# A routed and a dense mixture of experts behind linear attention: order of weight requests, scatters and weight sums

## The chip, the cores and the metric

The kernel runs on one core of one Trainium2 chip. The metric is the device time of one execution in microseconds (us). All inputs and outputs are float32; where a product goes to TensorE, both factors are split into a high and a low part, and three matmuls (high x high, high x low, low x high) stand for one.

## The reference

Three layers follow one another; N = 2304 rows, D = 512 columns, E = 8 experts, F = 1024.

```python
x = attention(q, k, v, w_phi)            # linear attention, 2304 x 512
# moe: some rows are computed, each by one expert
do_compute = x @ w_skip > 0
e_idx = argmax(x[do_compute] @ w_gate, axis=1)
x[do_compute] += gate_w * (relu(x @ w1[e]) @ w2[e])     # e = e_idx of the row
# moe2: every row by every expert
P = exp(x @ w_gate - max); 8 times: normalise rows, then columns
for e in range(8):
    out += P[:, e:e + 1] * (relu(x @ w1[e]) @ w2[e])
```

## The kernel before, in words

**Attention** fills about the first 215 us and leaves x in a DRAM table `x2d`. A router (lines around 440 to 530) writes for every computed row its place in a list `idx` by nine scatters on POOL (`rt.scatter`, L456); the list is sorted by expert and cut into slots of 256 rows.

**moe1** (L561 to L777) works through the slots. In a slot `s` (`slot_body`, L650 on) POOL scatters the results of slot s-1 into `x2d`, in two halves of 128 rows (`put`, L715); SP reads the number of the next expert, the list of the next slot's rows (L586) and its w1 (L617); POOL gathers these rows (`fetch_x`, L597). TensorE makes the first product in eight pieces `ph` (L668), while ACT and DVE split w2 (L629, L630). Then `ahead` requests the next w2 and splits the next w1, `turned` transposes the next slot's rows on TensorE (L643) with copies on ACT (L645) and DVE (L646), and `product` makes the second product for half 0 and half 1 (L707), each ending in a DVE add into the gathered rows (L711). Slots 0 and 1 are always run. The slots from 2 on are nested conditions (`chain`, L730); in each, `ahead` and `turned` stand inside a condition on there being a next slot, and the second half of the product inside one on the slot being full (`tc.If(nfull > s - 2)`, L690). Slot 0 is put in order by a planner from the program order; slot 1 and all later ones run in the order in which they are written (`tc.manual_schedule`). In this data nine slots run; slots 7 and 8 are not full. After the last slot the Else branch of the chain scatters the last results, and 24 transposes on a constant (`warm`, L775) stand between it and moe2.

While moe1 runs, `ahead2()` takes single steps of moe2's beginning, in a fixed order: load w1 of the first quad (L818); make Strassen-like sums of it on POOL (`sums_w1`, three operations at L830 to L832); seven splits (`w1_high` on ACT, L842, `w1_low` on DVE, L848; the second split has one more POOL operation, L850); load w1 of the second quad. Before, the first step comes after `rt.scatter()`, the sums at the end of slot 0's `ahead`, four splits between slot 0's two products, three in slot 1, and the second load after slot 1.

**moe2** (L780 on) has three passes of 768 rows each over 16 quarters of experts; one pass and quarter is a `quad` (48 in all), and the passes run through the weights forth, back and forth, so a pass begins with the weights with which the last one ended. A quad has two groups (`group`, L1082). A group makes the hidden layer by seven products `pa`, `pb`, `pd` (L1031), with the additions on DVE (L1101, L1116) and copies on ACT (L1039, L1047), and the three `piece`s of the quad before (second product `py`, L1067, twelve matmuls for each piece and quarter-block) lie between them as fill. In group 0 ACT and DVE split this quad's w2 (`w2_high` L1017, `w2_low` L1022) in four blocks; in group 1 they split the next quad's w1. SP issues the loads: `load_w1` into one buffer, `load_w2` into two buffers `r2`, blocks 0 and 1 at the end of the quad before, blocks 2 and 3 as soon as blocks 0 and 1 are split. In the last pass's first quads SP also stores the finished rows (`out`, L1080); at the end of the second quad from a pass's end it loads the next pass's x. Quads 0 to 2 are ordered by the planner, all later ones run as written. The requests stand at the end of `quad`:

```python
                if g and more:
                    load_w1(wid[n + 1] + 1)
                    load_w2(wid[n + 1], 0)
                    load_w2(wid[n + 1], 1)
```

Before quad 0, moe2 loads six blocks of 128 rows (L886) and turns them (`x_block`): four transposes (L893) into one bank `pt` of two, from which ACT copies one half and DVE the other (L896, L897).

Of the kernel before, what the change touches and what calls it, by code (L numbers as in the profile page):

```python
# [11 lines left out]
U32 = mybir.dt.uint32  # L12
# [13 lines left out]
NTOK = B * S  # L26
# [534 lines left out]
def moe1(tc, nc, c, rt, w1, w2, idx, x2d, second, route, ahead2):  # L561

    with ExitStack() as ctx:
# [73 lines left out]
        def turned(s, ps0=None):  # L637
            xg, xT = xgs[s % 3], xTs[s % 2]
            for a in range(2):
                pt = (ps0.tile([P, NKB, P], F32, name="pt", tag="W", bufs=4) if ps0  # L640
                      else ps.tile([P, NKB, P], F32, name="pt", tag="T"))
                for kb in range(NKB):
                    nc.tensor.transpose(pt[:, kb], xg[:, a, kb * P : kb * P + P], c["ident"])  # L643
                oh, ol = [t[:, :, a * P : a * P + P] for t in xT]
                nc.scalar.activation(oh, pt, AF.Copy)  # L645
                nc.vector.tensor_tensor(ol, pt, f32(oh), ALU.subtract)  # L646
# [5 lines left out]
        def slot_body(s):  # L652
            xT = xTs[s % 2]
            last = s == NSLOT + 1
            if s:
                put(s - 1, (0, 1))
            if s == 0:
                e = e1
            elif not last:
                e = fetch(s + 1)  # L660
            hh = pool.tile([P, NFB, SLOT], F32R, name="hh", tag="hh", bufs=1)
            hl = pool.tile([P, NFB, SLOT], F32R, name="hl", tag="hl", bufs=1)
            for f in range(NFB):
                ph = ps.tile([P, SLOT], F32, name="ph", tag="H", bufs=3)
                n = 0
                for wt, xt in ((w1h, xT[0]), (w1h, xT[1]), (w1l, xT[0])):
                    for kb in range(NKB):
                        nc.tensor.matmul(  # L668
                            ph, wt[:, kb, f * P : f * P + P], xt[:, kb], start=(n == 0), stop=(n == 11)
                        )  # L670
                        n += 1
                nc.scalar.activation(hh[:, f], ph, AF.Relu)
                nc.vector.scalar_tensor_tensor(hl[:, f], ph, 0.0, f32(hh[:, f]), ALU.max, ALU.subtract)
                split_w(w2h[:, f], w2l[:, f], r2[:, f])
            if s < 2:
                ahead(s, e)
                if s == 0:
                    ahead2()
            elif not last:
                with tc.If(nslots > s - 1):  # L680
                    ahead(s, e)
                    turned(s + 1)
            product(s, 0, hh, hl)
            if s < 2:
                if s == 0:
                    turned(1)
                for _ in range(4 if s == 0 else 3):
                    ahead2()
                product(s, 1, hh, hl, (lambda: turned(2)) if s else None)
            else:  # L690
                with tc.If(nfull > s - 2):
                    product(s, 1, hh, hl)

        def ahead(s, e):
            fetch2(e)
# [3 lines left out]
        def product(s, a, hh, hl, between=None):  # L699
            xg = xgs[s % 3]  # L700
            py = ps.tile([P, D], F32, name="py", tag="Y")
            n = 0
            for f in range(NFB):
                if between and f == NFB // 2:
                    between()
                for ht, wt in ((hh, w2h), (hl, w2h), (hh, w2l)):
                    nc.tensor.matmul(  # L707
                        py, ht[:, f, a * P : a * P + P], wt[:, f], start=(n == 0), stop=(n == 23)
                    )
                    n += 1  # L710
            nc.vector.scalar_tensor_tensor(  # L711
                xg[:, a, 0:D], py, xg[:, a, D : D + 1], xg[:, a, 0:D], ALU.mult, ALU.add
            )

        def put(s, halves):  # L715
            ix, xg = ixs[s % 3], xgs[s % 3]
            for a in halves:
                ins = nc.gpsimd.indirect_dma_start(
                    out=x2d[:, :],
                    out_offset=bass.IndirectOffsetOnAxis(ap=ix[:, a].bitcast(U32), axis=0),  # L720
                    in_=xg[:, a],
                    in_offset=None,
                    bounds_check=NTOK - 1,
                    oob_is_err=False,
                )
                for o in rt.gathers + rt.written:
                    tc.declare_no_dep(ins.ins, o.ins, reason="distinct rows")
                rt.written.append(ins)

        def chain(s):  # L730
            if s <= NSLOT + 1:
                with tc.If(nslots > s - 2) as more:
                    slot(s)
                    chain(s + 1)
                with more.Else():
                    put(s - 1, (1, 0))
            else:
                put(s - 1, (1, 0))

        es = rt.early_slots()  # L740
        first = [next(es)]
# [20 lines left out]
        w2h, w2l = [pool.tile([P, NFB, D], F32R, name=nm, bufs=1) for nm in ("w2h", "w2l")]  # L762
        xTs.append([pool.tile([P, NKB, SLOT], F32R, name=nm, bufs=1) for nm in ("xTh1", "xTl1")])
        route(lambda: ps.tile([P, D], F32, name="pr", tag="Y"))
        rt.scatter()
        ahead2()
        tabs.extend(rt.slots())
        slot_body(0)
        slot(1)
# [2 lines left out]
        nfull = nc.values_load(tn[0:1, 0:1], min_val=0, max_val=NSLOT)  # L772
        nslots = nc.values_load(tn[0:1, 1:2], min_val=0, max_val=NSLOT)
        chain(2)
        for _ in range(24):  # L775
            nc.tensor.transpose(warm, c["ident"], c["ident"])  # L776
    yield  # L777

# [1 line left out]
def moe2(tc, nc, c, w_gate, w1, w2, x2d, xtd, out):  # L780
# [6 lines left out]
    with ExitStack() as ctx:  # L787
# [98 lines left out]
            nc.sync.dma_start(xr, row(t, 0))  # L886
            return xr

        def transposed(xr, dst):

            pt = ps.tile([P, NKB, P], F32, name="pt", tag="T", bufs=2)
            for kb in range(NKB):
                nc.tensor.transpose(pt[:, kb], xr[:, kb * P : kb * P + P], c["ident"])  # L893
            (d, s), *more = dst(pt)
            nc.scalar.activation(d, s, AF.Copy)
            for d, s in more:  # L896
                nc.vector.tensor_copy(d, s)  # L897

        def logits(ps_, h, src):

# [31 lines left out]

        def x_block(xr, h, i):
            sl = slice(i * P, i * P + P)
            transposed(xr, lambda pt: [(xq[h, kh][:, :, sl], pt[:, 2 * kh : 2 * kh + 2]) for kh in range(2)])

        def x_logits(h):
            logits(0, h, lambda kb: xq[h, kb // 2][:, kb % 2])
# [221 lines left out]
        def quad(n):  # L1160
            ps_, e, q = quads[n]
            nxt = n + 1 < NQD and quads[n + 1][0] != ps_
            near = n + 4 < NQD and quads[n + 4][0] != ps_ and quads[n + 3][0] == ps_
            fresh = n == 0 or wid[n] != wid[n - 1]
            more = n + 1 < NQD and wid[n + 1] != wid[n]
            for g in range(2):
                high, low = [none] * 7, [none] * 7
                if n == 0:
                    fill = [lambda i=i: other_logits(*others[2 * g + i]) if i < 2 else None for i in range(3)]
                else:  # L1170
                    fill = [lambda i=i: piece(n - 1, g, i) for i in range(TB)]
                if g == 0:
                    if more:
                        sums_w1(wid[n + 1])
                    if fresh:
                        for b, k in enumerate((0, 1, 4, 5)):
                            high[k] = lambda b=b: w2_high(wid[n], b)

                            def lo(b=b):
                                w2_low(wid[n], b)  # L1180
                                if b < 2:
                                    load_w2(wid[n], b + 2)

                            low[k] = lo
                    if nxt:
                        for i, k in enumerate((2, 3, 6)):
                            low[k] = lambda i=i: sum_x(i)
                elif more:
                    for k in range(7):
                        high[k] = lambda k=k: w1_high(wid[n + 1], k)  # L1190
                        low[k] = lambda k=k: w1_low(wid[n + 1], k)
                elif nxt:
                    for k in range(7):
                        high[k] = lambda k=k: x_high(k)
                        low[k] = lambda k=k: x_low(k)
                lead = [lambda: x_logits(0), lambda: x_logits(1)] if n == 0 and g == 0 else ()
                group(n, g, fill, high, low, lead)
                if g and more:
                    load_w1(wid[n + 1] + 1)
                    load_w2(wid[n + 1], 0)  # L1200
                    load_w2(wid[n + 1], 1)
                if near and g:
                    load_xt(ps_ + 1)
                if n == 0 and g:
                    sinkhorn_start()
                if 1 <= n <= 2:
                    sinkhorn_step()
                    sinkhorn_step()
# [115 lines left out]
```

## Time and profile before

| what | us |
|---|---|
| median of three runs | 1990.36 (1989.43 to 1997.06) |
| the profiled execution's own time | 1988.57 |
| its span | 1986.9 |
| around the span | 1.67 |
| TensorE busy in the span | 1945.5 (98%) |
| VectorE, ScalarE, GpSimd busy | 1263.2, 882.6, 354.1 |
| TensorE's share of the chain that ended last | 73% |
| mean granted TensorE clock | 0.992 of full speed |

PE is TensorE, DVE VectorE, ACT ScalarE, POOL GpSimd, SP SyncE, which issues most DMAs; SPq, PEq, POOLq are the engines' sequencers. A timeline row is: start in us from the span's start, duration of the run of equal instructions, engine, line, operation, tile written <- tiles read, shape, how many; in brackets the idle time of the engine just ahead and what ended it. In a window row the columns are: from : to, its length, busy time (and instructions) of PE, PEld, DVE, ACT, POOL, the granted clock (PEclk, share of full speed), the share in which the DMA engines were busy, and GB/s.

### The profile page before, as it was taken

The page shows a single profiled execution, that of the slowest core. Times are in us where ns is not written, and L with a number is a line of the kernel's source. Part 1 is how long each engine was busy: PE and PEld are TensorE (multiplying, and loading weights), DVE is VectorE, ACT ScalarE, POOL GpSimd, SP SyncE. Part 2 cuts the span into 40 slices and gives each one's busy share as a digit, 9 for nine tenths or more (in the row PEclk, how much of TensorE's full clock was granted, in tenths as well). Part 3 has the DMA queues.
Part 4 walks back from the last instruction along what each step waited for, and adds up shares of the span by engine and source line. Part 5 has one row for each costly group of instructions (what it writes and reads, how often), then busy time and mean ns, then how long its engine had stood idle before and what let it go on. Part 6 is the DMA issues. An engine that isn't in the chain of part 4 may idle for free.

```text
span 1986.9 us, 32388 instructions
## 1 busy us (share of the span) xinstructions
PE 1945.5 (98%) x12602; PEld 1738.5 (88%) x12602; DVE 1263.2 (64%) x2182; ACT 882.6 (44%) x1682; POOL 354.1 (18%) x293
## 2 busy tenths in 40 slices
PE   9989999989999999999999999999999999999999
PEld 8978889966889889898889889998888989899997
DVE  5767876764866666666555656666565666666663
ACT  5756555545444434343343434344334434434441
POOL 2020332221121221212021121212202121221210
PEclk9999999999999999999999999999999999999999
DMA  7324577645122221222112121222202121221211
GB/s 184 98 63 153 117 282 223 203 142 164 45 73 65 63 80 48 85 83 77 57 60 75 54 85 43 85 65 95 75 32 90 48 85 58 70 78 50 85 54 43
DMA packets 132711, 180.79 MB, mean 91 GB/s; under 512 B 22530, under 2 KB 86274, under 8 KB 132544
## 3 DMA queue, kind: packets, MB, share of 16 engines
q1 hardware_dynamic: 128768, 171.22, 27.4%
q0 software_dynamic: 3616, 7.30, 1.1%
q8 instruction: 102, 1.67, 0.4%
q14 instruction: 65, 0.53, 0.1%
q10 hardware_dynamic: 160, 0.07, 0.0%
HBM read 163.85 MB, written 17.69 MB: 91 GB/s over the span
## 4 chain that ended last, share of the span: by engine, by line
PE 73%; DMA 2%; DVE 2%; ACT 1%; SPq 0%; issue 0%; ACTq 0%
PE py L1067 37%; PE pb L1031 15%; PE pd L1031 10%; PE pa L1031 9%; DMA r<-in_moe_w_dram 2%; PE pg L903 1%; PE pt L893 0%; DVE wcl L848 0%; SPq L818 0%; ACT w2h L1017 0%; PE warm L776 0%; DVE w2l L1022 0%; DVE hl L1052 0%; DMA xr<-x2d 0%; DVE acc L1078 0%
## 5 line engine op out<-in xcount | busy, mean ns | idle before, releaser
L1067 PE MATMUL py<-w2l,hh 128*128 128x512 f32 x1152 | 452.1, 393 | 0.0
L1067 PE MATMUL py<-w2h,hh 128*128 128x512 f32 x1152 | 451.8, 392 | 0.0
L1067 PE MATMUL py<-w2h,hl 128*128 128x512 f32 x1152 | 451.2, 392 | 0.0
L1022 DVE TENSOR_TENSOR w2l<-r,w2h 128x512 fp32r<-128x512 f32 x184 | 176.2, 963 | 207.4 <-ACT w2h L1017 207.3
L1067 PEld LDWEIGHTS py<-w2l,hh 128*128 128x128 f32 x1152 | 216.6, 188 | 48.4
L1067 PEld LDWEIGHTS py<-w2h,hl 128*128 128x128 f32 x1152 | 216.7, 188 | 38.7 <-issue 1.3
L1067 PEld LDWEIGHTS py<-w2h,hh 128*128 128x128 f32 x1152 | 216.9, 188 | 36.2
L1078 DVE SCALAR_TENSOR_TENSOR acc<-py,lg,acc 128x512 f32<-128x512 f32 x264 | 197.1, 747 | 68.4 <-PE py L1067 67.6
L1047 ACT ACTIVATE hh<-c 128x384 fp32r<-128x384 f32 x192 | 100.9, 525 | 214.1 <-DVE c L1116 119.4
L1017 ACT ACTIVATE w2h<-r 128x512 fp32r<-128x512 f32 x184 | 114.3, 623 | 171.5 <-DMA r<-in_moe_w_dram 171.2
L850 POOL TENSOR_TENSOR r<-r,s 128x512 f32<-128x512 f32 x46 | 59.7, 1297 | 667.6 <-DVE wcl L848 667.6
L830 POOL TENSOR_TENSOR s<-r 128x512 f32<-128x512 f32 x46 | 59.2, 1287 | 569.8 <-DMA r<-in_moe_w_dram 568.7
L1031 PE MATMUL pb<-xch,wch 128*128 128x384 f32 x576 | 149.9, 341 | 7.9 <-ACT v L1039 6.5
L848 DVE TENSOR_TENSOR wcl<-r,wch 128x512 fp32r<-128x512 f32 x230 | 154.2, 686 | 2.3 <-ACT wch L842 1.8
L1031 PE MATMUL pb<-xch,wcl 128*128 128x384 f32 x576 | 148.0, 337 | 0.0
L1031 PE MATMUL pb<-xcl,wch 128*128 128x384 f32 x576 | 147.8, 337 | 0.0
L842 ACT ACTIVATE wch<-r 128x512 fp32r<-128x512 f32 x230 | 138.6, 622 | 7.3 <-PE pa L1031 2.9
L1101 DVE TENSOR_TENSOR pb<-pb,s 128x384 f32<-128x384 f32 x96 | 54.4, 566 | 121.9 <-PE pb L1031 65.3
L1031 PEld LDWEIGHTS pb<-xch,wch 128*128 128x128 f32 x576 | 105.4, 188 | 28.2 <-ACT v L1039 12.3
L1039 ACT ACTIVATE s<-pa 128x384 f32<-128x384 f32 x96 | 47.2, 491 | 175.8 <-PE pa L1031 175.8
L1052 DVE SCALAR_TENSOR_TENSOR hl<-c,hh 128x384 fp32r<-128x384 f32 x192 | 106.6, 555 | 6.1 <-ACT hh L1047 6.1
L848 DVE TENSOR_TENSOR wcl<-s,wch 128x512 fp32r<-128x512 f32 x92 | 64.8, 704 | 70.6 <-ACT wch L842 69.4
(237 smaller groups left out, 3573.2 us busy)
## 6 DMA issues: line engine op xcount, KB each, us to landing
r<-in_moe_w_dram SPq DMA_DIRECT2D x168, 512.0 KB, 3.6
r<-in_moe_w_dram SPq DMA_DIRECT2D x184, 256.0 KB, 4.1
qt<-in_q_dram SPq DMA_DIRECT2D x16, 288.0 KB, 5.1
x2d<-x SPq DMA_DIRECT2D x4, 1152.0 KB, 5.5
xr<-x2d SPq DMA_DIRECT2D x18, 256.0 KB, 3.7
out_dram<-acc SPq DMA_DIRECT2D x18, 256.0 KB, 2.1
kt<-in_k_dram SPq DMA_DIRECT2D x16, 256.0 KB, 4.5
vs<-in_v_dram SPq DMA_DIRECT2D x14, 256.0 KB, 3.9
```

The source lines that it names most:

```text
L830: g.tensor_tensor(s1, a21, a22, ALU.add)
L842: nc.scalar.activation(wc[m, i][0], wsrc[m][i], AF.Copy)
L848: nc.vector.tensor_tensor(l, src[i], f32(h), ALU.subtract)
L850: nc.gpsimd.tensor_tensor(src[3], src[2], src[6], ALU.subtract)
L1017: nc.scalar.activation(h, w2r[m, b], AF.Copy)
L1022: nc.vector.tensor_tensor(l, w2r.pop((m, b)), f32(h), ALU.subtract)
L1031: nc.tensor.matmul(dst, w[:, kb, sl], x[:, kb], start=(start and m == 0), stop=(stop and m == 5), skip_group_check=True,)
L1047: nc.scalar.activation(hh, src, AF.Relu)
L1052: nc.vector.scalar_tensor_tensor(hl, src, 0.0, f32(hh), ALU.max, ALU.subtract)
L1067: nc.tensor.matmul(py, ht[:, i * P : i * P + P], wt, start=(m == 0), stop=(m == 11))
L1078: nc.vector.scalar_tensor_tensor(accs[t], py, lg[:, t, e : e + 1], accs[t], ALU.mult, ALU.add)
L1101: v.tensor_tensor(b, b, s, ALU.add)
```

## The change

- In moe2, blocks 0 and 1 of the next quad's w2 are requested at the end of group 0 and not of group 1; `load_w1` stays at the end of group 1, and so now comes behind them.
- `put` scatters one half. The second half's scatter is issued right behind the second half's product, inside its condition (in slots 0 and 1 without one); the next slot, or the Else branch, scatters half 0 alone. In a slot that isn't full, half 1 is no longer scattered.
- The load and the sums of moe2's first w1 go ahead of the router's nine scatters. Slot 0 takes three splits (the second with its POOL operation), slot 1 four.
- In slot 2, `turned(3)` moves out of its condition and behind the first half's product.
- 16 warm transposes stand where 24 stood.
- In `x_block`, both copies of a block go to ACT or both to DVE, by turns.

```diff
@@ slot_body
             if s:
-                put(s - 1, (0, 1))
+                put(s - 1, 0)
...
             if s < 2:
                 ahead(s, e)
-                if s == 0:
-                    ahead2()
             elif not last:
                 with tc.If(nslots > s - 1):
                     ahead(s, e)
-                    turned(s + 1)
+                    if s > 2:
+                        turned(s + 1)
             product(s, 0, hh, hl)
             if s < 2:
                 if s == 0:
                     turned(1)
-                for _ in range(4 if s == 0 else 3):
+                for _ in range(3 if s == 0 else 4):
                     ahead2()
                 product(s, 1, hh, hl, (lambda: turned(2)) if s else None)
+                put(s, 1)
             else:
+                if s == 2:
+                    turned(3)
                 with tc.If(nfull > s - 2):
                     product(s, 1, hh, hl)
+                    put(s, 1)
@@ chain
                 with more.Else():
-                    put(s - 1, (1, 0))
+                    put(s - 1, 0)
             else:
-                put(s - 1, (1, 0))
+                put(s - 1, 0)
@@ moe1
+        ahead2()
+        ahead2()
         rt.scatter()
-        ahead2()
...
-        for _ in range(24):
+        for _ in range(16):
             nc.tensor.transpose(warm, c["ident"], c["ident"])
@@ x_block
+            if (h + i) % 2:
+                transposed(xr, to, nc.vector.tensor_copy)
+            else:
+                transposed(xr, to)
@@ quad
                 if g and more:
                     load_w1(wid[n + 1] + 1)
+                elif more:
                     load_w2(wid[n + 1], 0)
                     load_w2(wid[n + 1], 1)
```

## Rows read from the trace of the kernel before

**Rows 1.** The chain that ended last, in order of time: start, duration, engine.

```profile
571.61 2.76 PE py L1067 x12
587.21 2.76 PE py L1067 x12
...
996.83 2.29 PE pb L1031 x6
999.12 4.50 PE py L1067 x12
1003.62 1.06 PE pb L1031 x6
...
1943.46 2.76 PE py L1067 x12
```

**Rows 2.** Waits of PE after 500 us: total, count, longest.

```profile
PE pb L1031 <- ACT v L1039: 6.5, 5, 3.3
PE pd L1031 <- DVE c L1116: 2.0, 2, 1.0
```

**Rows 3.** Timeline of SP and ACT at quad 17, the second quad of the second pass.

```profile
978.76 9.00 SPq L1080 DMA_DIRECT2D out_dram<-acc  x3
...
988.92 10.24 SPq L1013 DMA_DIRECT2D r<-in_moe_w_dram  x4
...
995.76 0.63 ACT L1017 ACTIVATE w2h<-r 128x512 fp32r<-128x512 f32 x1 [7.52 <-DMA r<-in_moe_w_dram]
```

**Rows 4.** Timeline of a quad in mid-pass: w2 requests (SP), the last block's split (DVE).

```profile
1717.50 9.43 SPq L1013 DMA_DIRECT2D r<-in_moe_w_dram  x4
...
1731.94 0.68 DVE L1022 TENSOR_TENSOR w2l<-r,w2h 128x512 fp32r<-128x512 f32 x1
```

**Rows 5.** Timeline of slot 0: first and last list scatter, last weight sum, split; slot 1's first matmuls.

```profile
224.24 1.02 POOL L456 DMA_INDIRECT idx<-ids,di  x1 [46.15 <-DVE n L524]
...
235.31 1.42 POOL L456 DMA_INDIRECT idx<-ids,di  x1 [0.30 <-issue]
...
241.62 1.26 POOL L832 TENSOR_TENSOR r<-r 128x512 f32<-128x512 f32 x1
241.68 0.63 ACT L842 ACTIVATE wch<-s 128x512 fp32r<-128x512 f32 x1 [7.95 <-POOL s L831]
...
243.34 0.73 PE L668 MATMUL ph<-xTh,w1h 128*128 128x256 f32 x4 [2.11 <-ACT xTh L645]
```

**Rows 6.** Windows: the beginning of slot 1.

```profile
244.80:248.40 3.60, 3.60 (x21) 3.60 (x20) 3.60 (x5) 1.10 (x3) 1.56 (x1) 0.53 0.24 49
```

**Rows 7.** Timeline of slot 1: list of slot 2's rows (SP), slot 2's first matmuls (PE).

```profile
251.21 0.39 SPq L586 DMA_DIRECT2D ix<-idx  x1
...
268.63 0.72 PE L668 MATMUL ph<-xTh,w1h 128*128 128x256 f32 x4
```

**Rows 8.** Timeline: a gather and the transposes that use it, in slots 2 and 4.

```profile
274.63 1.10 POOL L597 DMA_INDIRECT xg<-x2d,ix  x1 [0.31 <-issue]
...
281.78 0.63 PE L643 MATMUL pt<-ident,xg 128*128 128x128 f32 x4 [0.50 <-DMA xg<-x2d,ix]
...
321.39 1.01 POOL L597 DMA_INDIRECT xg<-x2d,ix  x1 [0.31 <-issue]
...
328.05 1.04 PE L643 MATMUL pt<-ident,xg 128*128 128x128 f32 x8
```

**Rows 9.** Timeline of the end of moe1 and the beginning of moe2.

```profile
425.56 1.00 POOL L718 DMA_INDIRECT x2d<-xg,ix  x1 [0.31 <-POOLq L732]
427.55 5.17 PE L776 MATMUL warm<-ident 128*128 128x128 f32 x23 [4.51 <-PEq L732]
```

**Rows 10.** Windows: the warm transposes, and the transposes of x behind them.

```profile
427.50:432.70 5.20, 5.15 (x24) 5.16 (x25) 0.00 (x0) 0.00 (x0) 3.75 (x3) 0.50 0.60 176
432.70:436.00 3.30, 2.31 (x19) 1.82 (x18) 1.27 (x3) 1.88 (x4) 0.00 (x0) 0.99 1.05 380
```

**Rows 11.** Waits of PE from 400 to 445 us: total, count, longest.

```profile
PE pt L893 <- DVE xq L897: 1.2, 3, 0.5
```

More of the change, by code (lines that the diff above doesn't have):

```diff
@@ L713, in product, with put @@
             )
-        def put(s, halves):
+        def put(s, a):
             ix, xg = ixs[s % 3], xgs[s % 3]
[L717 to L728, printed above, removed]
+            ins = nc.gpsimd.indirect_dma_start(
+                out=x2d[:, :],
+                out_offset=bass.IndirectOffsetOnAxis(ap=ix[:, a].bitcast(U32), axis=0),
+                in_=xg[:, a],
+                in_offset=None,
+                bounds_check=NTOK - 1,
+                oob_is_err=False,
+            )
+            for o in rt.gathers + rt.written:
+                tc.declare_no_dep(ins.ins, o.ins, reason="distinct rows")
+            rt.written.append(ins)
         def chain(s):
@@ L887, in load_x, with transposed @@
             return xr
-        def transposed(xr, dst):
+        def transposed(xr, dst, copy=lambda d, s: nc.scalar.activation(d, s, AF.Copy)):
             pt = ps.tile([P, NKB, P], F32, name="pt", tag="T", bufs=2)
@@ L893, in transposed @@
                 nc.tensor.transpose(pt[:, kb], xr[:, kb * P : kb * P + P], c["ident"])
[L894 to L897, printed above, removed]
+            for d, s in dst(pt):
+                copy(d, s)
         def logits(ps_, h, src):
@@ L934, in x_block @@
             sl = slice(i * P, i * P + P)
-            transposed(xr, lambda pt: [(xq[h, kh][:, :, sl], pt[:, 2 * kh : 2 * kh + 2]) for kh in range(2)])
+            to = lambda pt: [(xq[h, kh][:, :, sl], pt[:, 2 * kh : 2 * kh + 2]) for kh in range(2)]
+            if (h + i) % 2:
+                transposed(xr, to, nc.vector.tensor_copy)
+            else:
+                transposed(xr, to)
         def x_logits(h):
```

## The prediction

> **What bounds the kernel now.** I read the page's busy times first: TensorE is busy for 98% of the span, so a change can only win in the stretches in which PE stands or runs at the lower clock, and three parts of this one touch such stretches. Next I read the chain that ended last [rows 1]. In moe2 its groups follow one another at 587.21 - 571.61 = 15.60 us. From the group at 571.61 to the last one, at 1943.46, there are 87 groups; 87 x 15.60 = 1357.2, and the trace takes 1371.85. So 14.65 us of moe2 are not the rhythm of PE, and the search is for where they lie. PE's waits after 500 us [rows 2] name two places: `pb` behind ACT's copy `v`, 6.5 us in five waits, and `pd` behind DVE's `c`, 2.0 us. The largest single wait, 3.3, is the one at quad 17. There the timeline of the queues [rows 3] gives the cause: SP first issues three stores of finished rows (from 978.76, over 9 us), and requests w2 at 988.92 only; ACT stands 7.52 us at the first w2 split, which runs at 995.76; the copy `v` is queued behind that split, and PE behind `v`. PE then pays twice. After the pause it runs at the lower clock: in [rows 1] twelve `py` take 4.50 at 999.12 against 2.76 elsewhere, and six `pb` 2.29 at 996.83 against 1.06 at 1003.62, together 3.0 us. A wait and its clock: 3.3 + 3.0 = 6.3 us at one place.
>
> **A: w2 requested in mid-quad.** It removes the late request. In a quiet quad [rows 4] the four w2 requests begin at 1717.50, at the start of the quad that needs them, and the last of the blocks is split at 1731.94 + 0.68 = 1732.6. There are two buffers, both free by then, so in the new order the next quad's first two requests can go out at about 1732.6, and the next quad begins 2 x 15.60 after 1717.50, at 1748.7: 16 us of lead instead of none. In quad 17 the request also goes ahead of the second three stores, and of `load_w1`, which is the only thing that is queued behind it. `load_w1` keeps its place and is first used by POOL's sums, later than w2 was. The same four blocks are moved, split by the same instructions; nothing is added on ACT or DVE. Gain: 6.3 at quad 17, 3.2 in the other four waits for `v`, 2.0 in those for `c` (DVE's w2 splits stand ahead of `c` and start late with ACT's), together 11.5; of the remaining 14.65 - 11.5 = 3.15, which no wait names, I take half, since the small losses can be ACT's late splits as well as anything else. **13.1 us**; bounds: 6.3 (only the pass boundary) and 14.65 (all).
>
> **B: weight sums ahead of the list.** Before, POOL issues nine scatters between 224.24 and 236.73, then the three sums up to 241.62 + 1.26 = 242.88, and ACT's first split of a sum waits 7.95 for them; the copy that slot 1's first matmul needs is queued behind it, and PE waits 2.11 at 243.34 [rows 5] and then works 3.6 us at a granted clock of 0.53 [rows 6], worth 3.6 x 0.47 = 1.7. The sums now come first (POOL stood idle for 46.15 before the first scatter, so there is room, if the weights have landed), and this pause of 2.11 + 1.7 = 3.8 goes; that is the upper bound. But slot 2 is tied to something else: its list is loaded at 251.21, when all scatters have landed, and its first matmul runs 17.42 later, at 268.63 [rows 7], with w1's load, its splits and the transposes in between. ACT has one split more in this stretch than before. If the list is complete when it was, most of the 3.8 is lost again in front of slot 2; if the sums push the scatters back by all their 242.88 - 236.73 = 6.15, the list is that much later, and with the 1.7 kept the part costs 4.4. I take **1.3**, a third of the upper bound, since the POOL had room; bounds -4.4 and 3.8.
>
> **C: turned(3) behind product 0.** Its transposes wait for the gathers: before the second four PE stands 0.50, and these four take 0.63 where eight take 1.04 in slot 4, which comes to 0.11 more [rows 8]. The same again for the first four gives 1.2; behind a product of 24 matmuls the rows have landed. **1.1**; bounds 0.5 and 1.2. What is next late there is nothing that the timeline shows.
>
> **Half scatters.** In a full slot the second half's scatter, which waits for DVE's last add, now goes ahead of the first half's, and the gathers come behind both. At worst they are 1.33 later (1.01 + 0.31, the pace of [rows 8]). A gather issued by 321.39 + 1.01 = 322.40 is used at 328.05, 5.65 later; 4.3 would be left. The longest landing that the rows allow is slot 2's, where the transposes did wait: 281.78 - (274.63 + 1.10) = 6.05. I cost the move at **nothing**, since the 4.3 is what is left behind the eight `ph` and w1's splits and no wait of PE shows in slot 4 now; but by the longest landing it would be 6.05 - 4.3 = 1.7 short in each of the five full slots, 8.7 us. The sequencer of POOL already followed that condition, so no branch is new to it.
>
> **D: the end of moe1.** The last slots aren't full, so one scatter less stands at the end: 1.31 on POOL (1.00 at 425.56 and 0.31 ahead of it), and the x loads, which wait for the last one, come that much earlier. PE's warm transposes take 5.17 / 23 = 0.22 each [rows 9]; eight fewer free 1.8, and the transposes of x move up by the smaller of the two with what slack the landing had: 1.5. In `x_block`, copies split by block and not by half let ACT and DVE work on different banks; PE waits 1.2 there [rows 11], of which I take 1.0. Against this stands the clock. While PE does nothing but these transposes, from 427.5 to 432.7, the granted clock is 0.50 (1.2 GHz), and in the next window, in which the x transposes go on, 0.99 (2.4 GHz) [rows 10]. If the warm ones are 1.5 us shorter and the rise stays where it is, that much of the x transposes runs at half speed, a loss of up to 0.75, of which 0.5 falls in PE's busy share (2.31 of 3.30). **2.0**; bounds 0.5 and 3.0 (1.8 + 1.2).
>
> The Trainium skill (TensorE: Matmul & The Clock Gate, Part 4: PE-mode transpose) says that transpose mode does not count as PE busy for the clock. By it the eight could be dropped without any price in clock, and part D would be 2.5 and not 2.0. The trace disagrees: its clock rose after 5.2 us in which PE did transposes alone.
>
> **Sum.** 13.1 + 1.3 + 1.1 + 0 + 2.0 = 17.5 us. The profiled execution took 1988.57; 1988.57 - 17.5 = 1971.1. The median of the runs is 1.79 above that execution, so on the median's basis **1972.9**. Attention, the normalisation of P and the tail are not touched.
>
> **The rivals**, on the same basis (1990.36):
> - *The list is late.* The sums, now first on POOL, push the nine scatters, and slot 2 starts some 4.4 us later than now instead of 1.3 earlier: 5.7 less gain, 1978.6. For it: three operations of 1.3 to 3.5 us stand in the same queue, and slot 2 follows its list at once. Against it: POOL had 46 us to spare. 0.14.
> - *Only the pass boundary was w2.* The small losses in the other quads come from something else: A gives 6.3, 1979.7. For it: four of five waits for `v` are 0.8 us on average; against it: ACT's w2 splits wait for the load in quad after quad. 0.08.
> - *Gathers uncovered.* Five full slots wait 1.7 each: 1981.4. Against it stands the 5.65 of [rows 8]. 0.04.
> - *The request is no earlier in fact*, because SP or a buffer holds it in mid-quad: A gives nothing, 1986.0. Against it is the free buffer at 1732.6. 0.04.
> - *Slower than before*: POOL stands at the first sum, waiting for moe2's first w1, whose load is in SP's queue behind moe1's, and nine scatters stand behind it. From the list load (251.21) slot 2 moves one for one. It decides from where B's loss eats the other 16.2 us, a list load after 267.4. With one 30 us late the time is 1990.36 + 30 - 16.2 = 2004.2. For it: one engine and one queue, and no way past a waiting operation; against it: the load is requested before the scatters too, and a w2 block lands in some 7 us even when late (988.92 to 995.76). 0.02.
>
> **How the numbers follow.** Forecast 0.68, rivals 0.14, 0.08, 0.04, 0.04, 0.02. All upper bounds together (14.65 + 3.8 + 1.1 + 3.0) give 1967.8, all lower ones (6.3 - 4.4 + 0.5 + 0.5) 1987.5. The low end is 1967.0, that and the 0.9 by which the fastest run lies under the median; the high end is 1982.0, which takes in the first three rivals and leaves out the last two and part of the mixtures. A measurement of this kernel can tell 0.5%, some 10 us, from no change: faster means under 1980.4. The forecast, the first rival and most of the second lie there, 0.84; a fifth of the first two, the uncovered gathers and the void request are within, 0.14; the last rival, slower, 0.02.
>
> **What would show it.** A: no wait of `pb` for `v`; the wait of ACT for w2 near nothing; a step of 15.60 through the pass boundary, clock 1.00 there. B: no wait of 7.95 on ACT; the list's load against 251.21, slot 2's start against 268.63. C: no PE wait on gathers in slot 2. Scatter order: gathers about 1.3 later after product 1, and no wait of PE on them. D: 16 warm transposes, x loads earlier, fewer waits of `pt`. Wrong would be: a list load late by over 6 us, PE waits for gathers in full slots, or a group step over 15.60 between 571 and 1944 whose loss isn't explained by w2.

## The result, and the profile after

The changed kernel takes 1970.19 us in the median (1967.06 to 1971.88, six runs), the kernel before 1989.89 beside it; the ratio is 0.9897, with a 95% interval of 0.9875 to 0.9919, some 20 us less. The prediction said 1972.9 (1967 to 1982). The profiled execution took 1970.39, its span 1968.7 against 1986.9: 18.2 us less.

The page's busy times of the changed kernel:

```profile
PE 1935.7 (98%) x12594; PEld 1734.5 (88%) x12594; DVE 1237.2 (63%) x2182; ACT 888.5 (45%) x1682; POOL 322.0 (16%) x291
```

TensorE's share is what it was; DVE and POOL have become 26 and 32 us lighter, DVE with the same 2182 operations and POOL with 291 against 293 (last section). ACT's w2 splits, by the pages before and after, no longer stand for their loads:

```profile
L1017 ACT ACTIVATE w2h<-r 128x512 fp32r<-128x512 f32 x184 | 114.3, 623 | 171.5 <-DMA r<-in_moe_w_dram 171.2
...
L1022 ACT ACTIVATE w2h<-r 128x512 fp32r<-128x512 f32 x184 | 114.0, 621 | 2.4 <-DMA r<-in_moe_w_dram 2.2
```

Next the chain of the changed kernel, at the places of [rows 1], and PE's waits after 500 us, to set beside [rows 2]:

```profile
568.08 2.76 PE py L1072 x12
...
583.67 2.76 PE py L1072 x12
...
1925.27 2.76 PE py L1072 x12
```

```profile
PE pb L1036 <- ACT z L1044: 1.0, 1, 1.0
```

1925.27 - 568.08 = 1357.19, which is 87 x 15.60 to the last hundredth. All of moe2's 14.65 us are gone, and both waits with them; the one that is left lies in the planner's quads. The place of [rows 3], in the timeline of the changed kernel:

```profile
966.94 0.87 SPq L1018 DMA_DIRECT2D r<-in_moe_w_dram  x2
...
973.44 9.00 SPq L1085 DMA_DIRECT2D out_dram<-acc  x3
...
982.55 0.99 SPq L821 DMA_DIRECT2D r<-in_moe_w_dram  x2
...
982.83 0.62 ACT L1022 ACTIVATE w2h<-r 128x512 fp32r<-128x512 f32 x1
```

w2 is asked for 15.9 us before its first split, ahead of the second three stores, and the split carries no wait. Now slots 0 and 1 (to set beside [rows 5] and [rows 7]):

```profile
224.84 1.03 POOL L456 DMA_INDIRECT idx<-ids,di  x1 [46.04 <-DVE n L524]
...
236.33 1.30 POOL L835 TENSOR_TENSOR r<-r 128x512 f32<-128x512 f32 x1
...
240.72 0.97 POOL L456 DMA_INDIRECT idx<-ids,di  x1 [0.30 <-issue]
...
242.68 0.73 PE L668 MATMUL ph<-xTl,w1h 128*128 128x256 f32 x4 [1.69 <-DVE xTl L646]
...
248.71 0.38 SPq L586 DMA_DIRECT2D ix<-idx  x1
...
265.51 1.91 PE L779 MATMUL warm<-ident 128*128 128x128 f32 x16
267.18 0.72 PE L668 MATMUL ph<-xTh,w1h 128*128 128x256 f32 x4
```

```profile
242.60:246.20 3.60, 3.52 (x29) 3.52 (x30) 3.60 (x8) 1.75 (x4) 1.37 (x2) 1.00 0.19 75
```

ACT's wait of 7.95 has gone, and PE's 2.11 has become 1.69 for the low part of the turned rows; behind it the granted clock is 1.00, where it was 0.53 [rows 6]. The planner did not put the sums ahead of the scatters but between them: the last scatter is issued at 240.72 and not at 235.31. Yet the list is loaded at 248.71 and not at 251.21, 2.5 us earlier. And something stands here that the prediction didn't have: all 16 warm transposes, 1.67 us of PE ahead of slot 2, on a constant, long before the place for which they are written. Two more stretches, slot 2 and the end of moe1 (beside [rows 8] and [rows 9]):

```profile
269.44 1.29 POOL L833 TENSOR_TENSOR s<-r 128x512 f32<-128x512 f32 x1 [1.70 <-ACT hh L672]
...
278.19 1.01 POOL L597 DMA_INDIRECT xg<-x2d,ix  x1 [0.31 <-issue]
...
284.24 1.04 PE L643 MATMUL pt<-ident,xg 128*128 128x128 f32 x8
...
421.56 1.02 POOL L720 DMA_INDIRECT x2d<-xg,ix  x1 [12.74 <-POOLq L734]
...
427.68 1.09 PE L896 MATMUL pt<-ident,xr 128*128 128x128 f32 x4 [7.26 <-DMA xr<-x2d]
429.40 4.16 PE L896 MATMUL pt<-ident,xr 128*128 128x128 f32 x16 [0.63 <-DMA xr<-x2d]
```

The sums of moe2's second w1, which came behind moe1 before (427.56), now run in slot 2, ahead of the gathers; the transposes behind product 0 don't wait for them. At the end PE has nothing to do for 7.26 us, and 16 x transposes take 4.16 us, 0.26 each, against 0.14 (8 in 1.16) before, as PE is at half clock:

```profile
429.40:433.20 3.80, 3.76 (x16) 3.02 (x17) 1.45 (x5) 1.89 (x5) 0.00 (x0) 0.50 1.01 336
```

Slot 0's first matmul lies between 205 and 215 us in the profiled executions, whatever the kernel, so the table counts from there: from slot to slot by the first `ph` matmul of each, from slot 7 to moe2's first `pa`, and over 87 groups of moe2 by the `pa` that opens each. "List" is the load of slot 2's list after slot 0's first matmul. The ratio is to the kernel before on the same chip; each stretch is read from one profiled execution.

| kernel | ratio (95%) | list | slot 0 to 2 | 2 to 3 | 3 to 7 | 7 to moe2 | moe2 |
|---|---|---|---|---|---|---|---|
| before | 1 | 37.46 | 54.88 | 24.55 | 93.29 | 49.70 | 1371.85 |
| changed | 0.9897 (0.9875 to 0.9919) | 34.19 | 52.66 | 23.40 | 93.29 | 49.34 | 1357.20 |
| changed, once more | 0.9909 (0.9891 to 0.9927) | 35.45 | 53.28 | 23.40 | 93.29 | 48.91 | 1357.20 |
| w2_only | 0.9926 (0.9902 to 0.9950) | 35.95 | 54.66 | 24.30 | 93.29 | 49.16 | 1357.20 |
| w2_swap | 0.9925 (0.9906 to 0.9943) | 35.29 | 54.87 | 24.13 | 93.29 | 51.18 | 1357.20 |
| w2_bound | 0.9971 (0.9955 to 0.9987) | 35.02 | 54.64 | 24.20 | 93.29 | 49.80 | 1364.56 |
| no_w2 | 0.9987 (0.9976 to 0.9998) | 35.07 | 52.64 | 24.54 | 93.29 | 48.86 | 1372.34 |
| sums_late | 0.9930 (0.9910 to 0.9949) | 32.97 | 55.85 | 23.40 | 93.29 | 48.90 | 1357.20 |
| warm_none | 0.9907 (0.9888 to 0.9927) | 36.78 | 55.29 | 23.53 | 93.29 | 48.89 | 1357.20 |
| warm_pin16 | 0.9903 (0.9883 to 0.9924) | 34.79 | 50.95 | 24.66 | 93.29 | 48.34 | 1357.20 |
| put_old | 0.9916 (0.9897 to 0.9934) | 34.20 | 50.98 | 24.14 | 93.29 | 50.64 | 1357.20 |
| turned_in | 0.9921 (0.9904 to 0.9937) | 34.73 | 52.72 | 31.58 | 93.27 | 49.41 | 1357.20 |
| xblock_old | 0.9921 (0.9904 to 0.9937) | 35.04 | 52.67 | 23.40 | 93.29 | 49.31 | 1357.20 |
| mix | 0.9891 (0.9874 to 0.9907) | 34.79 | 51.02 | 23.84 | 93.29 | 49.39 | 1357.20 |

Between the two traces: 14.65 + 2.22 + 1.15 + 0 + 0.36 = 18.38 us less in these stretches, 0.57 less in the planner's quads, and 0.77 more ahead of slot 0. One pair is not enough for the stretch "7 to moe2": the four kernels that have moe1 as before (before, w2_only, w2_swap, w2_bound) take 49.16 to 51.18 there.

### The profile page after: what moved, and what is told of

The parts are those of the page before. It is cut to its first block, busy times and chain, and to the rows that moved or that the text cites. A ratio compares the mean times of both kernels' runs of the same rounds, so it can differ in the third digit from the quotient of the medians.

```text
span 1968.7 us, 32463 instructions
## 1 busy us (share of the span) xinstructions
PE 1935.7 (98%) x12594; PEld 1734.5 (88%) x12594; DVE 1237.2 (63%) x2182; ACT 888.5 (45%) x1682; POOL 322.0 (16%) x291
## 4 chain that ended last, share of the span: by engine, by line
PE 77%; DVE 1%; ACT 0%; DMA 0%; issue 0%; SPq 0%; ACTq 0%
PE py L1072 40%; PE pb L1036 15%; PE pa L1036 10%; PE pd L1036 10%; PE pg L904 1%; PE pt L896 1%; DMA xr<-x2d 0%; ACT acc L1220 0%; ACT wch L845 0%; PE pl L909 0%; PE pc L1002 0%; DVE lg L1007 0%; DVE w2l L1027 0%; DVE wcl L851 0%; DVE cs L1000 0%
## 5 line engine op out<-in xcount | busy, mean ns | idle before, releaser
L1027 DVE TENSOR_TENSOR w2l<-r,w2h 128x512 fp32r<-128x512 f32 x184 | 129.5, 705 | 71.9 <-ACT w2h L1022 71.9
L1044 ACT ACTIVATE z<-pb 128x384 f32<-128x384 f32 x96 | 47.1, 491 | 247.1 <-PE pb L1036 247.0
```

Of the source, the lines that this page charges most:

```text
L1027: nc.vector.tensor_tensor(l, w2r.pop((m, b)), f32(h), ALU.subtract)
L1044: nc.scalar.activation(t, src, AF.Copy)
```

## The experiments

**The w2 requests, four ways.** Alone, put back, turned round, and early at the pass boundaries only:

```diff
 # w2_only: the kernel before
                 if g and more:
                     load_w1(wid[n + 1] + 1)
+                elif more:
                     load_w2(wid[n + 1], 0)
...
 # no_w2: the changed kernel
-                elif more:
                     load_w2(wid[n + 1], 0)
...
 # w2_swap: the kernel before
                 if g and more:
-                    load_w1(wid[n + 1] + 1)
                     load_w2(wid[n + 1], 0)
                     load_w2(wid[n + 1], 1)
+                    load_w1(wid[n + 1] + 1)
 # w2_bound: the kernel before
+                if more and g == (0 if n in (16, 32) else 1):
                     load_w2(wid[n + 1], 0)
...
```

> The kernel before with one edit alone: blocks 0 and 1 of the next w2 requested at the end of group 0. Theory 1 (all that moe2 loses against a step of 15.60 is late w2): the groups run at 15.60 from the fourth quad to the end, moe2 is 14.65 us shorter, nothing else moves, about 1975.2 against 1989.9. Theory 2 (only the pause behind the three stores at quad 17 was w2, 6.3 us): 1983.6, and some ten groups stay longer than 15.60.

> The changed kernel with the w2 requests put back to the end of group 1, all its other edits kept. Theory 1: moe2 loses its 14.65 us again, and the rest keeps what the two traces show for it (2.2 up to slot 2, 1.2 in the slots, about 1 at moe2's start, less 0.8 that attention took longer by chance), about 1986. Theory 2 (the earlier edits also shift something in moe2, so that its waits come out otherwise): a loss in moe2 under 10 us, 1980 or less.

> The kernel before with the order at the end of group 1 turned round: w2's two requests, then w1's. They are issued 1 us earlier than before and no longer behind 1 MB of w1. Theory 1a (lead is what counts): ACT still waits about 3 us for w2 in every quad, the pause at quad 17 stays, the gain is under 4 us, 1986 or more. Theory 1b (w1's transfer ahead of w2's in the queues is what made w2 late): ACT's mean wait for w2 falls from 4.0 to under 2.5, and the loss outside the pass boundaries (about 6.4 of 14.65) goes, about 1983.

> The kernel before with the early request only in the first quad of the second and third pass, for quads 17 and 33; all other requests where they were. Theory 1: the losses in these two quads go (6.26 and 1.97), the others stay, 8.2 us, about 1981.7. Theory 2 (the pause at quad 17 only moves to the next quad with a late request): the groups after it lose what quad 17 gains, under 3 us in all, 1987 or more.

w2_only wins the 14.65 whole, no_w2 loses 15.14, w2_bound wins 1371.85 - 1364.56 = 7.29 of the 8.2 expected. So theory 1 of w2_only, no_w2 and w2_bound stands: the loss in moe2 comes and goes with w2's requests, whatever the rest of the kernel does. The surprise is w2_swap, of which neither theory comes true: its requests stand at the end of group 1 in the program, and moe2 loses nothing either. Its timeline, at quad 17 and in mid-pass:

```profile
979.54 0.88 SPq L1013 DMA_DIRECT2D r<-in_moe_w_dram  x2
980.52 0.93 SPq L818 DMA_DIRECT2D r<-in_moe_w_dram  x2
...
982.44 0.63 ACT L1017 ACTIVATE w2h<-r 128x512 fp32r<-128x512 f32 x1 [2.50 <-DMA r<-in_moe_w_dram]
...
1695.61 0.93 SPq L818 DMA_DIRECT2D r<-in_moe_w_dram  x2
1699.29 11.00 SPq L1013 DMA_DIRECT2D r<-in_moe_w_dram  x4
```

In mid-pass the four requests that SP issues in one stretch of 11.00 us are blocks 2 and 3 of this quad and blocks 0 and 1 of the next; w1 follows at the next quad's start. The changed kernel has the same pattern, w1 at 1698.60 and four of w2 from 1702.28 over 11.00 us. Before, the next in line was `load_w1`, whose one buffer is free only when group 1's last split has read it. SP's waits for it in the whole kernel before (total, count, longest):

```profile
SPq L818 <- DVE wcl L848: 904.2, 43, 26.8
```

So SP stands at w1's request for 21 us at a time, and w2's requests stand behind it with both their buffers free: since 1732.6 by [rows 4], while the next ones go out at 1748.91. Either edit puts them in front. Quad 17 tells what else matters: there w2_swap's requests do come behind all six stores, as before, and directly ahead of w1 instead of behind it. They land in 982.44 - 979.54 = 2.90 us, against 995.76 - 988.92 = 6.84 with w1's 1 MB in front [rows 3]; ACT waits 2.50, and PE not at all.

**The sums behind the scatters again.**

```diff
-        ahead2()
-        ahead2()
         rt.scatter()
+        ahead2()
...
                 ahead(s, e)
+                if s == 0:
+                    ahead2()
...
-                for _ in range(3 if s == 0 else 4):
+                for _ in range(4 if s == 0 else 3):
```

> The changed kernel with moe2's first load and sums behind the nine scatters again and the splits four and three. Theory 1 (what was won in slots 0 and 1 is the end of ACT's wait for the sums): ACT waits 6 us or more for a sum again, PE waits some 2 us at slot 1's start and runs at the lower clock behind it, slot 0 to slot 2 takes 54.9 us or more (16 transposes included), 2 us more in all. Theory 2 (the list decides, and the sums don't move it): 52.7 as it was.

```profile
233.78 0.63 ACT L846 ACTIVATE wch<-s 128x512 fp32r<-128x512 f32 x1 [11.94 <-POOL s L835]
...
235.43 1.22 PE L668 MATMUL ph<-xTh,w1h 128*128 128x256 f32 x4 [3.50 <-ACT xTh L645]
...
238.94 0.39 SPq L586 DMA_DIRECT2D ix<-idx  x1
```

Theory 1: ACT and PE wait for the sums again, and slot 0 to slot 2 takes 3.19 us more than in the changed kernel. The loss lies up to slot 1: from slot 0's first matmul to slot 1's it is 29.47 us, against 25.83 in the changed kernel and 29.59 in the kernel before. The list is the earliest of all (32.97), so it isn't the list that costs the time here.

**The warm transposes: none, and behind the last slot.** warm_none leaves the 16 out; warm_pin16 writes them into a bank of moe2, which ties them to moe1's end.

```diff
-        for _ in range(16):
-            nc.tensor.transpose(warm, c["ident"], c["ident"])
 # warm_pin16 only, ahead of the x blocks in moe2
+        wm = ps.tile([P, NKB, P], F32, name="wm", tag="T", bufs=2)
+        for i in range(16):
+            nc.tensor.transpose(wm[:, i % NKB], c["ident"], c["ident"])
```

> The changed kernel without its 16 warm transposes, which leave no result. In its trace they run between slot 1's last product and slot 2's first matmul, 1.67 us on PE. Theory 1 (PE is what slot 2's start hangs on): slot 0's first matmul to slot 2's first takes 51.0 and not 52.7 us, the end of moe1 is as it was, 1.7 us less in all. Theory 2 (slot 2 hangs on its list of rows, 18.5 us ahead of it): 52.7 as it was, PE waits in their place.

> The changed kernel with the 16 transposes written into a bank of moe2, so that they stand behind the last slot. Theory 1 (they bring the clock up, as 23 did in the kernel before): 51.0 us from slot 0 to slot 2; at the end the x transposes run partly at full clock, slot 7's first matmul to moe2's first takes 47.8 and not 49.3; 3.2 us less in all. Theory 2 (transposes don't bring the clock up): 51.0, and 49.9 at the end, since 16 transposes at half clock last 0.6 us beyond the moment at which the first x block has landed; 1 us less in all.

In warm_none the list came late (36.78), and its slot 1 shows the second road to slot 2's start:

```profile
243.30 0.39 SPq L586 DMA_DIRECT2D ix<-idx  x1
...
254.56 0.63 PE L643 MATMUL pt<-ident,xg 128*128 128x128 f32 x4 [0.52 <-DMA xg<-x2d,ix]
257.01 0.63 PE L643 MATMUL pt<-ident,xg 128*128 128x128 f32 x4 [1.82 <-DMA xg<-x2d,ix]
```

PE waits 2.3 us for the gathered rows, so this run can't tell what the transposes cost. warm_pin16, with its list at 34.79, can: 50.95, which is 52.66 - 1.71, as theory 1 has it. But 1.26 comes back at once: slot 2 to slot 3 takes 24.66 and not 23.40, as PE then waits 1.1 for slot 3's rows. At the end, PE's first transposes and two windows of its clock:

```profile
416.75 3.68 PE L1144 MATMUL wm<-ident 128*128 128x128 f32 x16 [4.04 <-DVEq L734]
```

```profile
420.20:422.00 1.80, 1.47 (x8) 1.10 (x7) 0.00 (x0) 0.66 (x2) 0.00 (x0) 0.50 1.00 356
422.00:424.50 2.50, 2.04 (x17) 1.62 (x15) 1.14 (x4) 1.47 (x4) 0.00 (x0) 0.95 1.00 347
```

PE does nothing but transposes from 416.75 to 424.4, and the granted clock goes from 0.50 (1.2 GHz) to 0.95 within them; in the changed kernel it is 0.50 in all of 427.6 to 433.2. The stretch is 1.0 us shorter (48.34), of 1.5 expected, but only 0.55 shorter than in warm_none (48.89), which has no such transposes anywhere; the ratio (0.9903) doesn't tell the kernel from the changed one. The Trainium skill (TensorE: Matmul & The Clock Gate, Part 4: PE-mode transpose) has transposes not count as PE busy for the clock; this run, like [rows 10], disagrees. They don't always bring it up: mix, further down, has 15 at the same place and stays at half clock.

**The scatters as before.** `put` takes both halves at the next slot's start and in the Else again.

```diff
-                put(s - 1, 0)
+                put(s - 1, (0, 1))
...
                     product(s, 1, hh, hl)
-                    put(s, 1)
...
-                    put(s - 1, 0)
+                    put(s - 1, (1, 0))
```

> The changed kernel with the scatters as before: both halves at the next slot's start, both in the Else. With them 15 of the 16 transposes come to stand behind the last slot again. Theory 1 (the second scatter at the end is 1.3 us on the way to the x loads, and the order within the slots costs nothing either way): slots 3 to 7 take 93.3 as in both traces; slot 0 to slot 2 51.1; slot 7 to moe2 between 48.5 and 50.5. Theory 2 (scatters at the slot's start hold the gathers back): slots 3 to 7 take 95 or more.

93.29 in slots 3 to 7, to the hundredth the time of every other kernel but turned_in (93.27): the order of the scatters costs nothing there. 50.98 to slot 2, with 15 of the 16 transposes back behind the last slot; and the sums of moe2's second w1 at 416.00, behind moe1. So it was the split of `put` that let the planner pull both forward. At the end the x loads are first asked for 42.10 us after slot 7's first matmul, as in the kernel before, and not 40.94: that 1.2 is the one scatter more. The stretch itself takes 50.64, just past the range expected; the 1.3 over the changed kernel is less than kernels with this end differ among themselves (49.16 to 51.18), and the transposes have moved too, so it can't be called the scatter's price.

**Slot 2's transposes back in their condition.**

```diff
-                    if s > 2:
-                        turned(s + 1)
+                    turned(s + 1)
...
-                if s == 2:
-                    turned(3)
```

> The changed kernel with the transposes for slot 3 back inside their condition, ahead of slot 2's first product. Theory 1 (the planner has moved the sums of moe2's second w1 in front of the gathers in slot 2, some 4.7 us on POOL, so this edit pays for more than the wait seen before): PE waits 3 us or more for the gathers, slot 2 to slot 3 takes 26.5 or more. Theory 2 (the edit is worth the 1.1 us that was forecast): 24.5.

```profile
276.90 1.01 POOL L597 DMA_INDIRECT xg<-x2d,ix  x1 [0.31 <-issue]
...
281.22 1.09 PE L643 MATMUL pt<-ident,xg 128*128 128x128 f32 x4 [4.87 <-DMA xg<-x2d,ix]
```

```profile
284.00:287.00 3.00, 3.00 (x8) 2.31 (x7) 0.69 (x1) 0.44 (x1) 0.00 (x0) 0.50 0.99 381
287.00:290.00 3.00, 3.00 (x14) 2.49 (x13) 0.00 (x0) 0.00 (x0) 0.00 (x0) 0.98 0.41 158
```

Theory 1, and more than it asked for: PE waits 5.3 us for rows that are gathered behind the sums, then works at half clock until about 287, and slot 2 to slot 3 takes 31.58, 8.2 more. In the medians it is 1973.79 against 1969.48 of the changed kernel beside it, 4.3; the profiled run was the longest of its four (1976.47), so 8.2 is more than the edit is usually worth.

**x_block's copies as before.** Each block's two halves go to ACT and DVE again.

```diff
-            if (h + i) % 2:
-                transposed(xr, to, nc.vector.tensor_copy)
-            else:
-                transposed(xr, to)
+            transposed(xr, to, None)
...
-            for d, s in dst(pt):
-                copy(d, s)
+            for i, (d, s) in enumerate(dst(pt)):
+                if copy is None and i:
+                    nc.vector.tensor_copy(d, s)
+                else:
+                    nc.scalar.activation(d, s, AF.Copy)
```

> The changed kernel with x_block's copies as before, one half on ACT and one on DVE. Theory 1 (with the x transposes at half clock in the changed kernel, the copies are no longer what they wait for): slot 7 to moe2 within 0.4 of 49.3. Theory 2 (as forecast, 1.0 us): 50.3, with waits of the transposes for DVE.

49.31 against 49.34 and 48.91: theory 1, nothing to be seen. The transposes wait 0.2 us for a copy in this run.

**A mix, and the changed kernel beside it.** Slots 0 and 1 scatter both halves at the next slot's start, later ones by halves.

```diff
             if s:
                 put(s - 1, 0)
+                if s < 3:
+                    put(s - 1, 1)
...
                 product(s, 1, hh, hl, (lambda: turned(2)) if s else None)
-                put(s, 1)
...
                 with more.Else():
+                    if s == 2:
+                        put(s - 1, 1)
                     put(s - 1, 0)
```

> The changed kernel, but slots 0 and 1 scatter both halves at the next slot's start as before; later slots by halves as changed. In its order of instructions 15 of the 16 transposes stand behind the last slot and no sums in front of slot 2's gathers. Theory 1 (what PE wins at slot 2's start is partly given back, as slot 3's w1 comes no earlier): slot 0 to slot 2 51.0, slot 2 to slot 3 24.1, slot 7 to moe2 48.5, some 1.8 us under the changed kernel. Theory 2 (nothing is given back): 51.0, 23.3 and 48.5, 2.6 us under it.

> The changed kernel once more, beside the three that follow. Slot 0 to slot 2 52.7, slot 2 to slot 3 23.4, slots 3 to 7 93.3, slot 7 to moe2's first matmul 49.3, no loss in moe2. Theory 1 (slot 2's start hangs on PE as long as the list is loaded within about 35.5 us of slot 0's first matmul, and on the list when it is later): 52.7 with an early list, up to 55.3 with a late one. Theory 2 (on PE alone): 52.7 in any case.

The changed kernel's second profile has the list at 35.45, 53.28 to slot 2 and a wait of 0.4 for the rows: the list begins to count at about 35 (xblock_old, at 35.04, has no such wait). mix takes 51.02, 23.84 and 49.39, by these stretches 1.15 less than the changed kernel, nearer to theory 1. Its end is 0.9 longer than expected. PE's x transposes there, and the window around them:

```profile
426.19 3.88 PE L899 MATMUL pt<-ident,xr 128*128 128x128 f32 x16 [0.73 <-DMA xr<-x2d]
```

```profile
426.20:429.70 3.50, 3.46 (x16) 3.07 (x17) 1.16 (x4) 1.53 (x4) 0.00 (x0) 0.50 0.98 355
```

PE does transposes alone from 420.96 to 429.7, with one wait of 0.73, and the clock is 0.50 all the time. In warm_pin16 the wait between the two kinds of transposes was 0.3, in the kernel before there was none; whether that is what decides is not shown. The ratio of mix is the lowest (0.9891), its median 1967.61 against 1969.48, but the intervals overlap, so it isn't shown to be faster.

## Why the prediction was right, step by step

- **A**, 13.1 forecast, 14.65 measured. The way from late w2 to ACT to `v` and `c` to PE held. The term mis-sized is the 3.15 that no wait named, of which half was taken: all of it was w2. The reason given for quad 17 was not the one that decides: the three stores delay the request, but w2_swap has them too, and PE doesn't wait. What decides is that w1's request stands in front: in mid-pass it holds w2's back, at quad 17 its 1 MB goes first. And it is the place in SP's queue that gives the lead of some 16 us, not the place in the program: w2_swap has it as well in mid-pass. At quad 17 it has none and PE doesn't wait; that the lead could be spared in every quad is not shown.
- **B**, 1.3 forecast, 2.22 measured in one pair of profiles and 1.6 with the second one (54.88 - 53.28). ACT's wait for the sums was the cause, as sums_late shows. The term mis-sized is the gain itself: from slot 0's first matmul to slot 1's it is 29.59 - 25.83 = 3.76, the whole upper bound of 3.8 and not a third of it. What is lost again, 1.54 from there to slot 2 (26.83 against 25.29), is the planner's 16 transposes and not the list; with them elsewhere (warm_pin16) it is 25.14. The step that failed is "slot 2 is tied to its list": in the changed kernel that holds only when the list is later than about 35 us, and in the kernel before, with the list at 37.46, PE's transposes of slot 2's rows didn't wait either:

```profile
264.99 1.04 PE L643 MATMUL pt<-ident,xg 128*128 128x128 f32 x8
...
268.60 0.27 PE L776 MATMUL warm<-ident 128*128 128x128 f32 x1
```

The first rival's premise came true, as the scatters were pushed back by 5 us, and its consequence didn't: the list was no later.
- **C**, 1.1 forecast, 1.15 measured in this pair, by another reckoning than the one given; that the two agree is luck. Without this edit the changed kernel waited 5.3 us in slot 2 (turned_in), as the sums stand before the gathers there. And "behind a product of 24 matmuls the rows have landed" doesn't hold in every run: no_w2, whose moe1 is the changed kernel's, takes 24.54 from slot 2 to slot 3, and warm_pin16 24.66 with a wait of 1.1. PE's waits for these rows in no_w2 (total, count, longest), behind the product:

```profile
PE pt L643 <- DMA xg<-x2d,ix: 0.7, 2, 0.5
```

The step "half scatters cost nothing" failed at this point: they cost nothing in slots 3 to 7, but their edit changed what the planner puts in slot 2.
- **D**, 2.0 forecast, 0.36 measured in this pair. The size isn't firm: the four kernels with moe1 as before take 49.16 to 51.18, mean 49.96, and five with the changed end (the changed kernel twice, no_w2, sums_late, turned_in) 48.86 to 49.41, mean 49.08, which makes 0.9. The scatter's part came where it was looked for: the x loads are first asked for 40.94 to 41.19 us after slot 7's first matmul in every kernel with the half scatters at the end, against 42.08 to 43.56. The steps that failed are the transposes and x_block: with no warm transposes at the end, PE waits for x and turns it at half clock (in mix it does so even with 15 of them there), and x_block's 1.0 isn't there (xblock_old). That 23 transposes stood in [rows 9] where the source has 24 was to be seen before: one of them ran already at 268.60 (in the lines under B), so the planner was free to move them.

- **The other rivals.** That only the pass boundary was w2 is out by w2_bound (7.29 of 14.65); gathers without cover by the 93.29; a request no earlier in fact by the 15.9 us of lead; POOL waiting for moe2's first w1 by the list, which came earlier.

The errors of A (1.55 too little), B (0.92 too little) and D (1.64 too much) nearly cancel, which is luck too; 17.5 were forecast, and 18.2 lie between the two spans.

## What to carry to other kernels

In these traces SP issued a DMA request not when the program reached it but when everything ahead of it in the queue had got its buffer (21 us on average in 43 waits at w1's request): look for a request with free buffers behind one whose buffer is busy, and put it in front. Work without data dependencies is no anchor in a planned stretch: an edit elsewhere can move it, as the split of `put` did. After each edit look where it went; a buffer of the place where it is wanted holds it there (warm_pin16), though that is not shown to have made this kernel faster. Where one edit hides another's damage (slot 2's transposes and the sums), only undoing them singly shows it.

## What the runs showed of the hardware

Late w2 had a second price, on engines that were not the bound. By the groups of lines from 600 to 1900 us, the kernel before:

```profile
L832 POOL TENSOR_TENSOR r<-r 128x512 f32<-128x512 f32 x39 | 68.0, 1744 | 0.0
...
L1022 DVE TENSOR_TENSOR w2l<-r,w2h 128x512 fp32r<-128x512 f32 x156 | 153.0, 986 | 192.4 <-ACT w2h L1017 192.2
```

and the changed kernel:

```profile
L835 POOL TENSOR_TENSOR r<-r 128x512 f32<-128x512 f32 x40 | 53.3, 1332 | 0.0
...
L1027 DVE TENSOR_TENSOR w2l<-r,w2h 128x512 fp32r<-128x512 f32 x160 | 111.0, 694 | 65.3 <-ACT w2h L1022 65.3
```

The same split takes 986 ns before and 694 after, the same sum 1744 and 1332. It goes with the order of w2's requests: from 590 to 1890 us the split takes 696 in w2_swap and 1020 in no_w2. The timeline of one quad before shows when:

```profile
1723.31 3.25 DVE L1022 TENSOR_TENSOR w2l<-r,w2h 128x512 fp32r<-128x512 f32 x2 [3.73 <-ACT w2h L1017]
...
1723.03 1.29 POOL L831 TENSOR_TENSOR s<-s,r 128x512 f32<-128x512 f32 x1
1724.28 1.74 POOL L832 TENSOR_TENSOR r<-r 128x512 f32<-128x512 f32 x1
```

Two splits beside POOL's sums take 3.25 us, where one without takes 0.68 [rows 4]. The Trainium skill (SBUF — State Buffer, Who interferes with whom) says that a DVE instruction with two SBUF inputs contends with a GpSimd one that reads SBUF, which this agrees with. And the list's landing doesn't follow its last scatter: issued at 235.31 before and 240.72 after, the list was loaded at 251.21 and 248.71. Why it varies from 33 to 37.5 us after slot 0's first matmul stays open.
